# Score products on quarters of the TensorE array, without the quarters that the mask covers, and two fixed PSUM tiles for attention

## The chip, the cores and the metric

The kernel runs on one core of one Trainium2 chip. The metric is the device time of one execution in microseconds; lower is better. The five engines of the core are called as the profile calls them: PE (TensorE, the matmuls; PEld is its weight loads), DVE (VectorE), ACT (ScalarE), POOL (GpSimd) and SP (SyncE, which here only issues DMAs).

A matmul on PE has two instructions. A weight load puts the stationary operand into the array, which has 128 rows (the contraction) and 128 columns (the partitions of the result); the matmul then streams the moving operand through it, column by column, and the result goes to PSUM, which has banks of 512 f32 per partition. `tile_position=(r, c)` places a product smaller than the array at row r and column c.

## The reference

Four layers in a row on one sequence of 2048 rows of 640 numbers: attention, feed-forward, attention, feed-forward, with the same weights both times. Attention has 32 heads of 20 numbers, and a query sees itself and the 255 keys before it:

```python
scores = jnp.einsum("bhqd,bhkd->bhqk", q, k) * (Dh ** -0.5)
mask = (idx[:, None] - idx[None, :] >= 0) & (idx[:, None] - idx[None, :] < W)   # W = 256
scores = jnp.where(mask[None, None], scores, -1e9)
p = _softmax(scores, axis=-1)
o = jnp.einsum("bhqk,bhkd->bhqd", p, v)
```

Each layer takes a layernorm of x and adds its result to x. The feed-forward is `relu(x @ w1 + b1) ** 2 @ w2 + b2`, with 1536 inner columns. All of it is f32.

## The kernel before

**Units and quads.** The 2048 rows are cut into 8 units of 256 rows (T), and the two attention layers make 16 units (NU), numbered u = 0 to 15; units 0 and 8 are the first of a layer and have no unit of keys before them. Within a unit, four heads make a quad (NQ = 8 quads a unit, 128 in all). A unit's queries see keys of their own unit and of the one before. The 256 rows are two blocks of 128, so keys come in four blocks: kb = 0, 1 of the unit before, 2, 3 of its own.

**Numbers in two halves.** f32 operands are split into two f16 parts (high and low), and the products high x high, high x low and low x high are added. In the large products this is three matmuls into one accumulator (`mm3`, L256). In the scores the three terms lie below each other in the contraction: 3 x 20 = 60 rows. So a score product fills only half of the array's rows, and a quad's four heads are laid out as two pairs: e = 0 on rows 0 to 63, e = 1 on rows 64 to 127, and j = 0, 1 for the two heads that share a half.

**The steps of a quad.**
- `max_quad` (L499 to L537) makes the maxima. For each of four windows w = 2 j + i (a head pair j and a block i of 128 queries) the queries are the weights and 384 keys stream past, for e = 0 and 1 (L523). The result, 128 queries x 384 keys, goes to the tile bb[e]: windows 0, 1, 2 to the first 384 columns of banks 0, 1, 2, window 3 to the last 128 columns of all three banks. The keys come from the tile of the unit before (`prev`) and of this unit (`cur`), so a window is two matmuls, window 3 three. DVE then adds the mask `maskb` and takes the row maximum (L535, eight times a quad). In a layer's first unit only the unit's own keys are there.
- `max_out` (L541 to L565) turns the maxima of two quads with a transpose on PE (L547), and DMAs them into two more rows of the query tile, so that the next product subtracts them: 62 rows.
- `exp_quad` (L570 to L624) makes the scores again, transposed: a block of 128 keys is the weights and 128 or 256 queries stream past (L585), for each step of `steps_of` (L626): key block 1 with both query blocks, key blocks 0 and 3 with one each, key block 2 with both. A step is one bank of bb[e] with up to 512 columns. ACT takes the exponent of the bank into `pt` (L598), and POOL sets the masked half of the blocks to zero (L613, L617).
- `pv_quad` (L633 to L668) multiplies by the values, four heads on four strips of 32 array columns (L647), in f32.

**The banks.** The two tiles bb (three banks each) serve the maxima and the exponents in turn. `banks()` (L494) is called at the start of each block: it lets the planner's clock pass until the jobs that read them are due to be done (`need(*bbjobs)`), and asks the pool for two tiles with `bufs=2`, which come to lie on the same two places each time. The code's framework sets the semaphores for them from what reads and writes which tile.

**The order of the work.** The order of instructions on each engine is that of the program, set by a planner written in the kernel: it counts an estimated clock `now[0]`, in which a score block of `max_quad` or `exp_quad` costs 870 ns, and posts jobs of DVE, ACT, POOL and SP (`post`, `pump`) when their inputs are due. `together` spreads a unit's score blocks and value products among the large products of the neighbouring units (the projections, wo, and the feed-forward, all at L256, called dense work here), so that PE goes through one list: dense work, a maximum block, the value products of another quad, dense work, an exponent block, dense work. In the last unit (u = 15) less dense work is left to put between.

Of the kernel before, what the change touches and what calls it, by code (L numbers as in the profile page):

```python
# [10 lines left out]
F32 = mybir.dt.float32  # L11
# [5 lines left out]
P = 128  # L17
# [4 lines left out]
DH = 20  # L22
# [22 lines left out]
def kernel(ctx: ExitStack, tc: tile.TileContext, x, wqkv, wo, w1, b1, w2, b2, out):  # L45
    nc = tc.nc
# [4 lines left out]
    ps = ctx.enter_context(tc.tile_pool(name="ps", bufs=1, space=bass.MemoryType.PSUM))  # L51
# [68 lines left out]
    def post(eng, cost, fn, *deps, wait=0.0, prio=1, **kw):  # L120

        j = Job(eng, cost, fn, [d for d in deps if d is not None], now[0] + wait, prio, **kw)
        k = len(pend)
        while k and pend[k - 1].prio > prio:
            k -= 1
        pend.insert(k, j)
        return j
# [18 lines left out]
    def pass_time():  # L146
        now[0] = max(now[0], min(k.start() for k in pend if k.ready()) - LOOK)
        pump()

    def need(*js):  # L150

        for j in js:
            while j.end is None:
                pass_time()
            now[0] = max(now[0], j.end)
# [174 lines left out]
    def ln_t(u, yT=None):  # L330
        ys = lns.pop(u)
        if yT is None:
            yT = sb.tile([P, 2, KC, T], F16, name="yT", tag="yT", bufs=1)
        yTs[u], pre[u] = yT, []
        bb = banks() if u == 0 else (None, None)
        for i in range(2):
            yield from split_t(ys[i][0], yT[:, :, :, i * P:(i + 1) * P], ys[i][1], pre[u], bb[i])
# [151 lines left out]
    GQ = NQ // 4  # L489
    mxs = {}  # L490

    bbjobs = []

    def banks():  # L494
        need(*bbjobs)
        bbjobs.clear()
        return [ps.tile([P, 3, 512], F32, name="bb", tag="bb", bufs=2) for e in range(2)]

    def max_quad(n):  # L499

        u, qd = divmod(n, NQ)
        g = u % NG
        qt, cur, prev = qts[u], kts[u % 3], kts[(u - 1) % 3]
        G = qd // GQ
        if (u, G) not in mxs:
            mxs[u, G] = sb.tile([P, 2, 2 * GQ, 2], F32, name="mx", bufs=2)
        mx = mxs[u, G]
        need(trips[u, 0, qd], trips[u, 1, qd])
        bb = banks()

        for w in (3, 0, 1, 2):
            j, i = divmod(w, 2)
            p = 2 * qd + j
            parts = [(prev, 0, T, 0), (cur, 0, P, T)] if i == 0 else [(prev, P, T, 0), (cur, 0, T, P)]
            if g == 0:
                parts = parts[1:]
            if w == 3:
                parts = [(kt, z, z + P, c + z - a) for kt, a, b, c in parts for z in range(a, b, P)]
            for kt, a, b, c in parts:
                for e in range(2):  # L520
                    r = slice(64 * e, 64 * e + 3 * DH)
                    to = bb[e][:, c // P, 3 * P:] if w == 3 else bb[e][:, w, c:c + b - a]
                    nc.tensor.matmul(to, qt[r, p, i * P:(i + 1) * P], kt[r, p, a:b], start=True, stop=True)  # L523
        now[0] += 870.0 if g else 440.0
        for w in range(4):
            j, i = divmod(w, 2)
            o = (0 if g else T if i == 0 else P)
            for e in range(2):
                accum = mx[:, e, (2 * qd + j) % (2 * GQ), i:i + 1]
                if w == 3:  # L530
                    v, mask = bb[e][:, o // P:, 3 * P:], maskb[:, o:].rearrange("p (a n) -> p a n", n=P)
                else:
                    v, mask = bb[e][:, w, o:3 * P], maskb[:, o:]
                bbjobs.append(post("D", 113 + 1.047 * (3 * P - o), lambda v=v, mask=mask, accum=accum:
                                   nc.vector.tensor_tensor_reduce(out=v, in0=v, in1=mask, scale=1.0, scalar=-3.0e38,  # L535
                                                                  op0=ALU.add, op1=ALU.max, accum_out=accum)))
        mxjobs[u, G] = list(bbjobs)  # L537
# [32 lines left out]
    def exp_quad(n):  # L570

        u, qd = divmod(n, NQ)
        qt = qts[u]
        bb = banks()
        steps = steps_of(u)
        if qd % GQ == 0:
            need(rowjobs.pop((u, qd // GQ)))
        for k, st in enumerate(steps):
            o = 0
            for kb, kt, ko, q0, qn in st:  # L580
                w = qn * P
                for j in range(2):
                    for e in range(2):
                        r = slice(64 * e, 64 * e + 3 * DH + 2)
                        nc.tensor.matmul(bb[e][:, k, o:o + w], kt[r, 2 * qd + j, ko:ko + P],  # L585
                                         qt[r, 2 * qd + j, q0 * P:q0 * P + w], start=True, stop=True)
                    o += w
        now[0] += 870.0 if u % NG else 530.0
        out, masks = [], []
        for k, st in enumerate(steps):  # L590
            pts, ms = [], []
            for e in range(2):
                o = sum(2 * qn * P for _, _, _, _, qn in st)
                box = {}

                def power(k=k, e=e, o=o, box=box):
                    box["pt"] = sb.tile([P, 512], F32, name="pt", tag="pt", bufs=6)
                    nc.scalar.activation(box["pt"][:, :o], bb[e][:, k, :o], AF.Exp, scale=SCALE / (QS * QS))  # L598

                ex = post("A", 50 + 0.834 * o, power)  # L600
                bbjobs.append(ex)
                o2 = 0
                for kb, kt, ko, q0, qn in st:
                    w = qn * P
                    part = slice(o2, o2 + 2 * w)
                    o2 += 2 * w

                    def mask(box=box, part=part, kb=kb, w=w):
                        pj = box["pt"][:, part].rearrange("p (j n) -> p j n", j=2)
                        if kb < 2:  # L610

                            m = pj[:, :, w - P:w]
                            nc.gpsimd.affine_select(out=m, in_=m, pattern=[[0, 2], [-1, P]],  # L613
                                                    compare_op=ALU.is_gt, fill=0.0, base=0, channel_multiplier=1)
                        else:
                            m = pj[:, :, 0:P]
                            nc.gpsimd.affine_select(out=m, in_=m, pattern=[[0, 2], [1, P]],  # L617
                                                    compare_op=ALU.is_ge, fill=0.0, base=0, channel_multiplier=-1)

                    ms.append(post("G", 375, mask, ex))  # L620
                    pts.append((e, kb, q0, qn, box, part))
            out.append(pts)
            masks.append(ms)
        return out, masks  # L624

    def steps_of(u):  # L626

        cur, prev = kts[u % 3], kts[(u - 1) % 3]
        if u % NG == 0:
            return [[(2, cur, 0, 0, 2)], [(3, cur, P, 1, 1)]]  # L630
        return [[(1, prev, P, 0, 2)], [(0, prev, 0, 0, 1), (3, cur, P, 1, 1)], [(2, cur, 0, 0, 2)]]
# [276 lines left out]
    def together(ns, ms, dense, cost, share=1.0, whole=True, after=None, pace=0):  # L908
# [5 lines left out]
        for k, (part_, what, m) in enumerate(ts):  # L914
            if what and what[0] == "s":
                quad = exp_quad(what[1])
                for it in late:
                    max_out(*it)
                late.clear()
            if m is not None:  # L920
                max_quad(m)
                if m % GQ == GQ - 1:
                    late.append((m // NQ, m % NQ // GQ))
            if what and what[0] == "v":
                pv_quad(what[1], quad)
            if after and k == 0:
                after()
            part += part_
            while done < cost * share * part / total:
                c = next(dense, None)  # L930
                if c is None:
                    break
                step(c)
                done += c
            if what is None:
                for it in late:
                    max_out(*it)
                late.clear()
# [114 lines left out]
```

## Time and profile before

| what | value |
|---|---|
| median of 3 runs | 1659.74 us (1657.5 to 1660.65) |
| span of the profiled execution, first to last instruction | 1660.5 us |
| PE busy | 1595.4 us, 96% of the span |
| mean granted TensorE clock | 0.986 |
| dense matmuls at L256 on the chain that ended last | 65% of the span |
| value products at L647 on it | 10% |
| exponent score products at L585 on it | 6% |
| maximum score products at L523 on it | 5% |

The profile is one execution on the chip; it gives no time of its own beside the span, and the span lies within the runs' times. PE's busy time counts matmuls that overlap once, and the ends of matmuls are modelled, so the argument goes by the starts of instructions in the timeline and not by busy shares. A row of the timeline merges instructions of one line that follow each other: start in us, length in us from the first start to the last end, engine, line, operation, out<-in, shape, and xcount. A row of the groups has the count, then the busy time in us, the mean length of one in ns, and the engine's idle time before them with what ended it.

### The profile page before, as it was taken

The page shows a single profiled execution, that of the slowest core. Times are in us where ns is not written, and L with a number is a line of the kernel's source. Part 1 is how long each engine was busy: PE and PEld are TensorE (multiplying, and loading weights), DVE is VectorE, ACT ScalarE, POOL GpSimd, SP SyncE. Part 2 cuts the span into 40 slices and gives each one's busy share as a digit, 9 for nine tenths or more (in the row PEclk, how much of TensorE's full clock was granted, in tenths as well). Part 3 has the DMA queues.
Part 4 walks back from the last instruction along what each step waited for, and adds up shares of the span by engine and source line. Part 5 has one row for each costly group of instructions (what it writes and reads, how often), then busy time and mean ns, then how long its engine had stood idle before and what let it go on. Part 6 is the DMA issues. An engine that isn't in the chain of part 4 may idle for free.

```text
span 1660.5 us, 44547 instructions
## 1 busy us (share of the span) xinstructions
PE 1595.4 (96%) x17574; PEld 1173.0 (71%) x17574; DVE 1032.8 (62%) x3231; ACT 750.1 (45%) x1616; POOL 636.8 (38%) x1309
## 2 busy tenths in 40 slices
PE   7787899999999999999999999999999999999989
PEld 5564676777777777777777777777777777776667
DVE  7566657675665766566565756657665666757341
ACT  4455534535444454544434354444545444453512
POOL 1343533524344353424414243443534344353512
PEclk9897999999999999999999999999999999999999
DMA  8465214343452534335153433424343352421020
GB/s 245 129 179 155 61 61 107 63 118 84 100 101 60 125 69 113 78 102 118 50 136 74 123 82 104 98 68 118 73 109 80 104 115 50 108 70 53 26 64 17
DMA packets 231484, 157.42 MB, mean 95 GB/s; under 512 B 79468, under 2 KB 215020, under 8 KB 231276
## 3 DMA queue, kind: packets, MB, share of 16 engines
q1 hardware_dynamic: 231276, 154.59, 37.8%
q8 instruction: 138, 2.26, 0.6%
q14 instruction: 70, 0.57, 0.1%
HBM read 84.68 MB, written 52.95 MB: 83 GB/s over the span
## 4 chain that ended last, share of the span: by engine, by line
PE 87%; DVE 5%; ACT 3%; DMA 3%; issue 1%; SPq 1%; POOL 0%; DVEq 0%; ACTq 0%; POOLq 0%
PE acc L256 65%; PE pv L647 10%; PE bb L585 6%; PE bb L523 5%; DVE bb L535 2%; ACT pt L598 2%; DMA qk<-qd 1%; PE tr L547 1%; DMA qk<-yl 0%; DMA w_s<-in_A_wqkv_dram 0%; DVE mx L535 0%; DMA ov<-o 0%; DMA qt<-qk 0%; ACT r L816 0%; SPq L560 0%
## 5 line engine op out<-in xcount | busy, mean ns | idle before, releaser
L535 DVE CUSTOM_DVE_ANT_0 bb<-bb,maskb 128x384 f32<-128x384 f32 (+2 forms) x1024 | 510.4, 565 | 117.3 <-PE bb L523 109.4
L598 ACT ACTIVATE pt<-bb 128x512 f32<-128x512 f32 (+1 forms) x736 | 376.5, 602 | 239.9 <-PE bb L585 239.6
L613 POOL TENSOR_SCALAR_AFFINE_SELECT pt<-pt 128x256 f32<-128x256 f32 x448 | 195.0, 440 | 542.8 <-ACT pt L598 521.4
L256 PE MATMUL acc<-y,w_s 128*128 128x256 f16 x2880 | 331.8, 273 | 4.2 <-DVE y L304 1.4
L256 PE MATMUL acc<-w_s,hh 128*128 128x320 f16 x2304 | 326.2, 299 | 0.0
L256 PEld LDWEIGHTS <-w_s 128*128 128x128 f16 x2880 | 278.5, 98 | 58.2 <-issue 25.7
L256 PE MATMUL acc<-yT,wq_s 128*128 128x256 f16 x2400 | 282.7, 276 | 12.6 <-DVE qd L414 10.6
L256 PEld LDWEIGHTS <-hh 128*128 128x128 f16 x2304 | 221.8, 98 | 97.8 <-issue 15.3
L256 PEld LDWEIGHTS <-wq_s 128*128 128x128 f16 x2400 | 233.7, 99 | 58.0 <-issue 27.8
L617 POOL TENSOR_SCALAR_AFFINE_SELECT pt<-pt 128x256 f32<-128x256 f32 x512 | 217.1, 446 | 64.3 <-ACT pt L598 63.2
L826 DVE TENSOR_TENSOR hh<-r,hh 128x256 f16<-128x256 f32 x192 | 91.7, 499 | 208.4 <-ACT hh L823 200.9
L647 PE MATMUL pv<-pt,vt 128*32 128x128 f32 (+1 forms) x3840 | 188.8, 331 | 2.0 <-POOL pt L617 1.4
L820 POOL TENSOR_TENSOR r<-r 128x256 f32<-128x256 f32 x192 | 113.5, 612 | 184.9 <-ACT r L816 183.4
L659 ACT COPY ot<-pv 128x256 f32<-128x256 f32 x128 | 47.6, 372 | 285.6 <-PE pv L647 285.6
L535 DVE DVE_READ_ACCUMULATOR2_ANT mx<- 128x1 f32 x1024 | 142.7, 139 | 0.1
L256 PE MATMUL acc<-wq_s,yT 128*128 128x320 f16 x960 | 142.0, 301 | 0.1
L647 PEld LDWEIGHTS pv<-pt,vt 128*32 128x32 f32 x3840 | 104.2, 110 | 49.1 <-issue 17.6
L256 PE MATMUL acc<-wo_s,od 128*128 128x320 f16 x900 | 131.9, 301 | 3.6 <-DVE x L758 1.7
L816 ACT ACTIVATE r<-acc,b1s 128x256 f32<-128x256 f32 x192 | 80.6, 471 | 99.8 <-PE acc L256 98.4
L256 PEld LDWEIGHTS <-yT 128*128 128x128 f16 x960 | 93.0, 98 | 40.4 <-issue 7.0
L585 PE MATMUL bb<-qt,kt 62*128 62x128 f16 (+1 forms) x1920 | 109.4, 246 | 10.6 <-DVE mx L535 9.8
L256 PEld LDWEIGHTS <-od 128*128 128x128 f16 x900 | 86.1, 98 | 45.9 <-issue 11.1
(84 smaller groups left out, 1175.7 us busy)
## 6 DMA issues: line engine op xcount, KB each, us to landing
qt<-qk SPq DMA_DIRECT2D x30, 480.0 KB
kt<-qk SPq DMA_DIRECT2D x30, 480.0 KB
qk<-qd SPq DMA_DIRECT2D x17, 640.0 KB
o<-ot SPq DMA_DIRECT2D x256, 42.0 KB
od<-o SPq DMA_DIRECT2D x13, 640.0 KB
qk<-yl SPq DMA_DIRECT2D x13, 640.0 KB
qk<-qd SPq DMA_DIRECT2D x17, 320.0 KB
xt<-in_A_x_dram SPq DMA_DIRECT2D x16, 320.0 KB
```

The lines of the kernel that those rows point to most:

```text
L256: nc.tensor.matmul(acc, lhs(a, c), rhs(b, c), start=(k == 0), stop=(k == 3 * nk - 1))
L523: nc.tensor.matmul(to, qt[r, p, i * P:(i + 1) * P], kt[r, p, a:b], start=True, stop=True)
L535: nc.vector.tensor_tensor_reduce(out=v, in0=v, in1=mask, scale=1.0, scalar=-3.0e38, op0=ALU.add, op1=ALU.max, accum_out=accum)))
L585: nc.tensor.matmul(bb[e][:, k, o:o + w], kt[r, 2 * qd + j, ko:ko + P], qt[r, 2 * qd + j, q0 * P:q0 * P + w], start=True, stop=True)
L598: nc.scalar.activation(box["pt"][:, :o], bb[e][:, k, :o], AF.Exp, scale=SCALE / (QS * QS))
L613: nc.gpsimd.affine_select(out=m, in_=m, pattern=[[0, 2], [-1, P]], compare_op=ALU.is_gt, fill=0.0, base=0, channel_multiplier=1)
L617: nc.gpsimd.affine_select(out=m, in_=m, pattern=[[0, 2], [1, P]], compare_op=ALU.is_ge, fill=0.0, base=0, channel_multiplier=-1)
L647: nc.tensor.matmul(pv[32 * jj:32 * (jj + 1), q0 * P:(q0 + qn) * P], vf[:, c:c + 32], pj[:, j, :], start=(k == 0), stop=(k == len(steps) - ...
L659: nc.scalar.copy(ot[:, qd % 2], pv)
L816: nc.scalar.activation(box["r"], acc[:, f, :], AF.Relu, bias=b1s[:, f0 + f:f0 + f + 1], scale=1.0 / (YS * WS))
L820: nc.gpsimd.tensor_tensor(box["r"], box["r"], box["r"], op=ALU.mult)
L826: nc.vector.tensor_sub(hh[:, 1, f, :], box["r"], hh[:, 0, f, :])
```

## The change

A score product now fills a quarter of the array: rows by e as before, and columns by a new half h = 0, 1. In `max_quad` h is a half of the 128 queries; in `exp_quad` it is a half of the 128 keys. Each quarter is a weight load of 64 columns and a matmul of its own, at `tile_position=(64 * e, 64 * h)`, whose result goes to 64 of the 128 partitions of bb[e].

From unit 2 on each half streams only what the mask leaves for some row of it. In `max_quad` the first 64 queries of a block see the first 320 of the window's 384 keys, the others the last 320. In `exp_quad` a half of a key block of the unit before (kb < 2) leaves out the last 64 queries if h = 0, and a half of a key block of its own unit leaves out the first 64 if h = 1. Units 0 and 1 are written whole. What is not written keeps what an earlier block left there; the mask of DVE and the zeros of POOL cover it as before.

`by_turns` orders the matmuls of the two halves: the next one comes from the half that has streamed fewer columns so far, and each is issued for e = 0 and e = 1.

The two tiles bb are made once, before the loop, and `banks()` returns them each time. The estimates (870 ns) and all jobs of the other engines are as they were.

```diff
+    def by_turns(ways):
+        t = [0, 0]
+        ways = [list(w) for w in ways]
+        while ways[0] or ways[1]:
+            h = min((h for h in range(2) if ways[h]), key=lambda h: t[h])
+            part = ways[h].pop(0)
+            t[h] += part[0]
+            yield h, part
+
     bbjobs = []
+    bbs = [ps.tile([P, 3, 512], F32, name="bb", tag="bb", bufs=2) for e in range(2)]
 
     def banks():
         need(*bbjobs)
         bbjobs.clear()
-        return [ps.tile([P, 3, 512], F32, name="bb", tag="bb", bufs=2) for e in range(2)]
+        return bbs
...
+            ways = [[], []]
             for kt, a, b, c in parts:
+                for h in range(2):
+                    lo, hi = (0, 3 * P) if u < 2 else (64 * h, 64 * h + 320)
+                    x, y = max(a, a + lo - c), min(b, a + hi - c)
+                    if x < y:
+                        ways[h].append((y - x, kt, x, y, c + x - a))
+            for h, (_, kt, a, b, c) in by_turns(ways):
                 for e in range(2):
-                    r = slice(64 * e, 64 * e + 3 * DH)
-                    to = bb[e][:, c // P, 3 * P:] if w == 3 else bb[e][:, w, c:c + b - a]
-                    nc.tensor.matmul(to, qt[r, p, i * P:(i + 1) * P], kt[r, p, a:b], start=True, stop=True)
+                    r, m = slice(64 * e, 64 * e + 3 * DH), slice(64 * h, 64 * h + 64)
+                    to = bb[e][m, c // P, 3 * P + c % P:3 * P + c % P + b - a] if w == 3 else bb[e][m, w, c:c + b - a]
+                    nc.tensor.matmul(to, qt[r, p, i * P + 64 * h:i * P + 64 * h + 64], kt[r, p, a:b],
+                                     start=True, stop=True, tile_position=(64 * e, 64 * h))
...
+        ways = [[], []]
         for k, st in enumerate(steps):
             o = 0
             for kb, kt, ko, q0, qn in st:
                 w = qn * P
                 for j in range(2):
-                    for e in range(2):
-                        r = slice(64 * e, 64 * e + 3 * DH + 2)
-                        nc.tensor.matmul(bb[e][:, k, o:o + w], kt[r, 2 * qd + j, ko:ko + P],
-                                         qt[r, 2 * qd + j, q0 * P:q0 * P + w], start=True, stop=True)
+                    for h in range(2):
+                        a, b = 0, w
+                        if u >= 2:
+                            a, b = (0, w - 64 * (1 - h)) if kb < 2 else (64 * h, w)
+                        ways[h].append((b - a, kt, 2 * qd + j, ko, q0 * P + a, k, o + a))
                     o += w
+        for h, (w, kt, p, ko, q, k, o) in by_turns(ways):
+            for e in range(2):
+                r = slice(64 * e, 64 * e + 3 * DH + 2)
+                nc.tensor.matmul(bb[e][64 * h:64 * h + 64, k, o:o + w], kt[r, p, ko + 64 * h:ko + 64 * h + 64],
+                                 qt[r, p, q:q + w], start=True, stop=True, tile_position=(64 * e, 64 * h))
```

## The prediction

> **What bounds the kernel now.** I read the shares and the chain on the page first, then the span cut into stretches, then single blocks in the timeline.
>
> ```profile
> span 1660.5 us, 44547 instructions
> ...
> PE 1595.4 (96%) x17574; PEld 1173.0 (71%) x17574; DVE 1032.8 (62%) x3231; ACT 750.1 (45%) x1616; POOL 636.8 (38%) x1309
> ...
> PE 87%; DVE 5%; ACT 3%; DMA 3%; issue 1%; SPq 1%; POOL 0%; DVEq 0%; ACTq 0%; POOLq 0%
> PE acc L256 65%; PE pv L647 10%; PE bb L585 6%; PE bb L523 5%; DVE bb L535 2%; ACT pt L598 2%; DMA qk<-qd 1%; PE tr L547 1%; DMA qk<-yl 0%; DMA w_s<-in_A_wqkv_dram 0%; DVE mx L535 0%; DMA ov<-o 0%; DMA qt<-qk 0%; ACT r L816 0%; SPq L560 0%
> ```
> ```profile
> 200.00:900.00 700.00, 695.88 (x7876) 516.08 (x7876) 445.99 (x1419) 319.20 (x697) 275.67 (x586) 1.00 0.39 92
> 900.00:1428.00 528.00, 526.91 (x6003) 390.35 (x6001) 346.53 (x1065) 240.19 (x517) 207.16 (x441) 1.00 0.39 93
> 1428.00:1574.00 146.00, 136.93 (x1596) 96.69 (x1595) 87.25 (x282) 68.48 (x152) 66.19 (x139) 0.99 0.24 60
> ```
> In the table of stretches the columns are length, then busy time of PE, PEld, DVE, ACT and POOL, granted clock, DMA share and GB/s. From 200 to 1428 us PE is busy 1222.8 of 1228 us at full clock: there PE is the limit, and a nanosecond taken off a score block is a nanosecond off the span, because PE works through one list in order. The two score blocks that the change rewrites (L585 and L523) are only 11% of the chain, some 180 us.
>
> ```profile
> 603.49 0.84 PE L523 MATMUL bb<-kt,qt 60*128 60x128 f16 x18
> 604.26 1.51 PE L647 MATMUL pv<-pt,vt 128*32 128x256 f32 x32
> ...
> 607.89 2.34 PE L256 MATMUL acc<-w_s,hh 128*128 128x320 f16 x16
> ...
> 610.16 0.83 PE L585 MATMUL bb<-qt,kt 62*128 62x256 f16 x16
> ...
> 610.93 5.06 PE L256 MATMUL acc<-w_s,hh 128*128 128x320 f16 x36
> ```
> ```profile
> L256 PE MATMUL acc<-w_s,hh 128*128 128x320 f16 x2304 | 326.2, 299 | 0.0
> L647 PE MATMUL pv<-pt,vt 128*32 128x256 f32 x1920 | 154.3, 388 | 0.3
> ```
> Sixteen 320-column matmuls take 2.34 us, and the last one's own length is 0.30, so they start (2.34 - 0.30) / 15 = 0.136 us apart: **0.425 ns per column**. A maximum block sends 4 x 384 = 1536 columns through each of its two row halves, an exponent block 6 x 256 = 1536. That is 0.653 us of streaming, if the halves run together. The timeline has the next work starting 0.77 us after either block starts (603.49 to 604.26, 610.16 to 610.93). The halves do run together: one after the other they would need 1.31 us. Streaming sets the block, and some 0.12 us go to its start and to the change of the array's division.
>
> **The change, part by part.** *Columns.* From unit 2 on, a query half needs 320 of 384 keys and a key half 192 of 256 queries (or 64 of 128) in a masked piece. Each quarter then streams 4 x 320 = 1280 columns, and an exponent quarter 512 + 384 + 384 = 1280 as well. That is 256 fewer per quarter, 256 x 0.425 = 109 ns per block. It holds where a block spans two key units: units 2 to 7 and 9 to 15, 13 x 8 = 104 quads, 208 blocks. Units 0 and 1 are written in full. In unit 8 one half keeps all its 768 columns while the other drops to 512, and the longer half sets the end. So 48 blocks (24 quads) gain nothing.
>
> *Instructions.* The 2176 matmuls of L523 become 4352 and the 1920 of L585 become 3840, each with its weight load: 36 for 18 and 32 for 16 in a full block. Four must run at once for the time above, and every load must hide behind the matmul before it in its own quarter. No row has such a quarter; the nearest ones are these.
>
> ```profile
> 604.26 0.42 PE L647 MATMUL pv<-pt,vt 128*32 128x256 f32 x4
> ```
> ```profile
> L523 PEld LDWEIGHTS <-qt 60*128 60x128 f16 x2176 | 72.7, 95 | 38.9 <-issue 35.7 <-DMA w_s<-in_A_wo_dram 0.3
> L647 PEld LDWEIGHTS pv<-pt,vt 128*32 128x32 f32 x3840 | 104.2, 110 | 49.1 <-issue 17.6 <-POOL pt L617 6.5 <-POOL r L820 1.9
> L300 PEld LDWEIGHTS tr<-ident,xt 128*128 128x128 f32 x50 | 5.5, 140 | 9.7 <-issue 3.5 <-DVE yT L304 1.8 <-ACT vt L480 1.7
> L547 PEld LDWEIGHTS tr<-ident,mx 128*16 128x16 f32 x64 | 5.6, 87 | 13.8 <-issue 8.8 <-DVE yl L414 2.9 <-PE acc L256 0.6
> ```
> *Four at once.* Four value products on four column strips span 0.42 us when one lasts 0.39: they start about 10 ns apart and overlap. Column strips overlap there, row halves overlap in the score blocks; both together is my assumption. A group of four that starts one by one costs some 15 ns more than today's pair at each block's start.
>
> *Loads.* Loads of 16 and 128 columns last 87 and 140 ns, so 53 / 112 = 0.47 ns per column over a fixed 79.5. That fixed part is latency. The 128-column f16 load has 95 - 79.5 = 15.5 ns beyond it, a fourth of what 0.47 would make, so today's loads take a quick form. The 32-column load on a strip has 110 - 79.5 = 30.5, which is 0.95 per column, twice the rate, but on f32. For 64 f16 columns the ends are therefore 64 x 0.12 = 8 ns and 64 x 0.95 = 61 ns; 0.47 gives 30. I take **30 ns**: the strip's row is nearer in its division of the array, but its f32 operand is wider, and the whole-array pair brackets 64 columns without that. At 30 ns the loads hide behind matmuls of 128 columns and more (54 ns) and barely fail behind those of 64 (27 ns). [...]
>
> *Sum.* A trimmed block: -109 + 15 + 15 + 20 = -59 ns; times 208 is -12.3 us. An untrimmed one: +15 + 15 + 10 for the order, times 48 is +1.9 us. Net **-10.4 us**.
>
> *Fixed banks.* The two bb tiles already fall on the same two buffers at every call, and the planner's clock (870 ns a block) and its list are untouched, so the order of emission stays.
>
> ```profile
> PE bb L585 <- DVE mx L535: 9.8, 10, 3.5
> ...
> PE bb L523 <- ACT pt L598: 4.3, 10, 1.2
> ```
> All waits of PE for the banks (columns: us, times, longest) are 14.1 us in 20 places. The first products into a bank still need its readers gone, and the last maximum of a quad (w = 3) reads all three banks. I put the gain at 0; the ends are -14 (all gone) and some +2 us, if more semaphores have to be asked for. DVE and ACT keep every instruction; they start when a block ends, earlier by what it saves, and the next score block comes earlier by as much, so their slack stays. Should DVE's eight maxima become late, the same bank wait grows.
>
> 1660.5 - 10.4 = 1650.1. The median, 1659.74, lies 0.8 us below the profiled span, within the 3.2 us between the runs; I say **1650.5 us**.
>
> **The rivals.**
> (a) *The load sets the pace* (slower). At 61 ns a quarter's nine matmuls in a maximum block (128, 128, 64, 256, 64, 128, 192, 256, 64 columns) cost six times 61 and 109, 82, 109, so 666 ns, and 61 for the first load: 727 + 15 against 668 today, +74. [...] It decides from a load of about 36 ns, where the 109 ns are used up. For it: the strip's row. Against it: the 16 and 128 column rows.
> (b) *The gain is used up.* A load of 33 to 39 ns, or some more cost at the start: 1660, within 0.2% either way.
> (c) *A floor per matmul, or quarters that take turns.* The closest steady spacing in the block row is 18 in 0.65 us, so about 36 ns, or 27 within its 128-column run. With 27 as a floor, 36 matmuls need 0.97 us and 32 need 0.86: some +0.25 us for each of 256 blocks, +64 us, 1725. Halves that took turns would add more still. Against it: four strip products started within 0.03 us. [...]
> (d) *Better than forecast.* Loads as quick as today's: -109 + 15 per trimmed block, -18 us in all, or the bank waits gone on top of the forecast: 1638 to 1643.
>
> **How the numbers follow.** Forecast 48%, (a) 21%, (b) 12%, (c) 10%, (d) 9%. A measurement here tells about 0.2%, 3.3 us, from no change. Faster: the forecast and (d), 0.57. Same: (b), 0.12. Slower: (a) and (c), 0.31. The forecast's own range, with a load of 27 to 33 ns, is 1646 to 1656. The 8-in-10 range runs from 1639, in (d), through the likeliest, (b) and most of (a), to 1690; it leaves out (c) and the edges of (a) and (d).
>
> **What will show it.** 4352 and 3840 score matmuls in the groups. The new loads' mean, less 79.5: 30 right, 50 or more means (a), 15 means (d). Start of a block to start of what follows: 0.71 us instead of 0.77 in units 2 and later, 0.81 in unit 1. Span from 200 to 1428 us down by some 10, as much as the blocks' sum; if the blocks shrink and the span doesn't, PE waits elsewhere and my one-to-one rule is wrong. The waits for DVE mx and ACT pt near 14 us. What would make all this wrong: four quarters not running at once.

## The result, and the profile after

The changed kernel takes 1642.91 us (median of 4 runs, 1641.93 to 1644.1) against 1659.74 (1657.5 to 1660.65). The ratio is 0.9899 with a 95% interval of 0.9885 to 0.9913: 16.8 us faster. The forecast was 1650.5, 9.2 us faster. The sign held, and the time lies in the stated range of 1639 to 1690, but near its lower end and outside the forecast's own range of 1646 to 1656: the gain is larger than the sum behind it.

The page of the changed kernel, the same lines as before:

```profile
span 1640.2 us, 52819 instructions
...
PE 1575.6 (96%) x21670; PEld 1172.6 (71%) x21670; DVE 1030.1 (63%) x3231; ACT 748.4 (46%) x1616; POOL 636.6 (39%) x1309
...
PE 83%; DVE 6%; ACT 4%; DMA 4%; POOL 2%; issue 1%; SPq 1%; DVEq 0%; ACTq 0%; POOLq 0%
```

PE has 4096 matmuls and as many weight loads more, and is busy 20 us less. DVE, ACT and POOL kept their counts. The table of stretches (length, then busy time of PE, PEld, DVE, ACT, POOL, granted clock, DMA share, GB/s) and the list of what PE waited for (us, times, longest):

```profile
200.00:900.00 700.00, 696.42 (x9795) 521.90 (x9793) 450.61 (x1439) 319.71 (x699) 275.43 (x584) 1.00 0.39 93
900.00:1428.00 528.00, 526.25 (x7608) 394.35 (x7606) 351.80 (x1086) 242.80 (x524) 208.93 (x447) 1.00 0.41 97
```
```profile
PE bb L613 <- DVE mx L555: 8.4, 11, 3.0
...
PE bb L542 <- ACT pt L625: 4.5, 10, 1.2
```

PE is as full as before (1222.7 of 1228 us): it is still the limit, and the same list passes in less time. The bank waits are 12.9 us in 21 places, against 14.1 in 20. So the gain is not in waits but in the blocks themselves. The timeline of PE in unit 6, where L523 is now L542 and L585 is L613:

```profile
631.61 0.76 PE L542 MATMUL bb<-kt,qt 60*64 60x128 f16 x36
632.29 1.51 PE L674 MATMUL pv<-pt,vt 128*32 128x256 f32 x32
...
637.65 0.75 PE L613 MATMUL bb<-qt,kt 62*64 62x192 f16 x32
638.34 0.28 PE L567 MATMUL tr<-ident,mx 128*16 128x128 f32 x1
```

From the start of a block to the start of what follows it takes 0.68 and 0.69 us, where it took 0.77. To the nanosecond of the trace the medians over units 2 to 7 and 9 to 14 (96 blocks of each kind) are 766 before and 685 after for both kinds, and a block also begins 3 ns sooner after the matmul ahead of it: **84 ns per trimmed block**.

The stage in which PE is the limit can be cut out cleanly, between the first exponent block of unit 2 and that of unit 15. Before:

```profile
238.14 0.28 PE L585 MATMUL bb<-qt,kt 62*128 62x256 f16 x1
```
```profile
1500.02 0.28 PE L585 MATMUL bb<-qt,kt 62*128 62x256 f16 x2
```
After:

```profile
234.24 0.27 PE L613 MATMUL bb<-qt,kt 62*64 62x192 f16 x1
```
```profile
1481.92 0.30 PE L613 MATMUL bb<-qt,kt 62*64 62x192 f16 x4
```

That stage took 1261.9 us and takes 1247.7: **14.2 us** of the gain. It came out the same to 0.1 us in two profiles of the changed kernel and 1.0 us apart in the widest pair of one program (e7_unit1 and e12_unit1 below), while the start of the kernel scatters by 2 us and the runs by 3; so the experiments below are read by it first and by their medians second. Its 192 trimmed blocks of 84 ns make 16.1 us. Three things take most of the difference: unit 8's 16 blocks are 13 to 20 ns longer (0.3 us), blocks that held a wait before shrink by less (0.7 us), and dense work now waits for DVE's reading of the transposed maxima, a wait that the stage of before does not have (0.9 us in this profile, 0.5 in the second one):

```profile
PE acc L256 <- DVE mT L573: 0.9, 3, 0.4
```

### The profile page after: what moved, and what is told of

It is laid out like the page before. It is cut to its first block, busy times and chain, and to the rows that moved or that the text cites. A ratio compares the mean times of both kernels' runs of the same rounds, so it can differ in the third digit from the quotient of the medians.

```text
span 1640.2 us, 52819 instructions
## 1 busy us (share of the span) xinstructions
PE 1575.6 (96%) x21670; PEld 1172.6 (71%) x21670; DVE 1030.1 (63%) x3231; ACT 748.4 (46%) x1616; POOL 636.6 (39%) x1309
## 4 chain that ended last, share of the span: by engine, by line
PE 83%; DVE 6%; ACT 4%; DMA 4%; POOL 2%; issue 1%; SPq 1%; DVEq 0%; ACTq 0%; POOLq 0%
PE acc L256 63%; PE pv L674 10%; PE bb L542 5%; PE bb L613 5%; DVE bb L555 3%; ACT pt L625 2%; DMA qk<-qd 1%; DMA xt<-in_B_b_dram 1%; PE tr L567 1%; POOL x L805 1%; DVE mx L555 1%; POOL pt L644 0%; ACT r L843 0%; DMA w_s<-in_B_w_dram 0%; DMA ov<-o 0%
## 5 line engine op out<-in xcount | busy, mean ns | idle before, releaser
L843 ACT ACTIVATE r<-acc,b1s 128x256 f32<-128x256 f32 x192 | 80.6, 471 | 98.0 <-PE acc L256 97.2
L613 PE MATMUL bb<-qt,kt 62*64 62x128 f16 (+3 forms) x3840 | 100.3, 235 | 9.1 <-DVE mx L555 8.4
```

Of the source, the lines that this page charges most:

```text
L613: nc.tensor.matmul(bb[e][64 * h:64 * h + 64, k, o:o + w], kt[r, p, ko + 64 * h:ko + 64 * h + 64], qt[r, p, q:q + w], start=True, stop=True ...
L843: nc.scalar.activation(box["r"], acc[:, f, :], AF.Relu, bias=b1s[:, f0 + f:f0 + f + 1], scale=1.0 / (YS * WS))
```

## The experiments

Each run was timed beside the kernel before on the same chip. "Stage" is the stretch just named.

| run | median, us | ratio to before (95%) | stage, us |
|---|---|---|---|
| before | 1659.7 to 1660.6 | 1 | 1261.9 |
| the change | 1642.9 | 0.9899 (0.9885 to 0.9913) | 1247.7 |
| e1_banks | 1660.1 | 0.9997 (0.9987 to 1.0007) | 1261.9 |
| e2_whole | 1663.1 | 1.0017 (1.0009 to 1.0026) | 1266.3 |
| e3_max_only | 1651.5 | 0.9947 (0.9933 to 0.9961) | 1255.6 |
| e4_exp_only | 1650.6 | 0.9944 (0.9931 to 0.9957) | 1254.7 |
| e5_cut64 | 1683.6 | 1.0138 (1.0123 to 1.0154) | 1282.3 |
| e6_in_turn | 1674.6 | 1.0078 (1.0064 to 1.0093) | 1271.4 |
| e7_unit1 | 1645.2 | 0.9904 (0.9890 to 0.9917) | 1249.6 |
| e8_estimate | 1650.0 | 0.9935 (0.9923 to 0.9948) | 1248.6 |
| e9_plain_order | 1643.3 | 0.9900 (0.9885 to 0.9916) | 1247.7 |
| e10_estimate950 | 1646.9 | 0.9917 (0.9904 to 0.9930) | 1246.1 |
| e11_changed | 1644.3 | 0.9909 (0.9892 to 0.9925) | 1247.7 |
| e12_unit1 | 1643.4 | 0.9903 (0.9888 to 0.9917) | 1248.7 |

### The fixed banks alone

```diff
+    bbs = [ps.tile([P, 3, 512], F32, name="bb", tag="bb", bufs=2) for e in range(2)]
...
-        return [ps.tile([P, 3, 512], F32, name="bb", tag="bb", bufs=2) for e in range(2)]
+        return bbs
```

> The kernel before with the two fixed bank tiles alone; all products as before. Theory (the gain is the columns that are not streamed, banks nothing): no change, within 1.5 us of before, the waits of PE for DVE mx and ACT pt still near 14 us. Rival (the fixed tiles let matmuls start before the last reader of the other banks is done): 5 to 14 us faster, and those waits shrink by as much.

The median and the stage are those of before. What PE waited for in this run:

```profile
PE bb L587 <- DVE mx L537: 9.3, 12, 3.0
...
PE bb L525 <- ACT pt L600: 4.4, 10, 1.2
```

13.7 us in 22 places: nothing moved. The rival is out, and all of the gain belongs to the products.

### Quarters without the trimming

```diff
-                    lo, hi = (0, 3 * P) if u < 2 else (64 * h, 64 * h + 320)
+                    lo, hi = 0, 3 * P
...
-                        if u >= 2:
-                            a, b = (0, w - 64 * (1 - h)) if kb < 2 else (64 * h, w)
```

> The changed kernel, with the quarters but without the trimming: every half streams all keys and queries in every unit. Theory: the division costs what it costs in unit 1 of the changed kernel, +44 ns for a maximum block and +20 ns for an exponent block, so about +32 ns for 256 blocks, 6 to 8 us slower than before (1666 to 1668). Rival (dividing the array is itself quicker, for instance by a shorter drain): faster than before, by up to half of the 16.8 us.

2.8 us slower than before (1.5 to 4.3). Dividing the array does cost, and nothing of the gain comes from it. It costs less than I expected: two blocks of this run, in PE's timeline,

```profile
622.49 0.85 PE L611 MATMUL bb<-qt,kt 62*64 62x256 f16 x32
623.28 0.28 PE L567 MATMUL tr<-ident,mx 128*16 128x128 f32 x1
...
628.37 0.86 PE L542 MATMUL bb<-kt,qt 60*64 60x128 f16 x36
629.16 1.08 PE L672 MATMUL pv<-pt,vt 128*32 128x256 f32 x24
```

take 0.79 us each (medians 787 and 786 ns), 20 more than before for both kinds. The +44 ns in my expectation was the median of the eight maximum blocks of unit 1 of the changed kernel. Four of them took 787 ns there too; the others took 882 to 1427 ns, and the two longest ran while the granted clock was 0.50. Against this run the trimming alone shortens a block from 787 to 685, 102 ns of the 109 that its columns make, and the stage by 18.6 us.

### One kind of block at a time

Each of these has the new code in one function, and the old lines in the other.

> The maxima in trimmed quarters, the exponent products as before. Theory: 104 blocks shorter by 84 ns and 24 longer by some 30, so 8 us faster than before (1652), half of the whole gain. Rival (the chain through the banks is the limit, so a shorter maximum block only makes the exponent block wait for DVE): less than 4 us.

> The exponent products in trimmed quarters, the maxima as before. Theory: 104 blocks shorter by 84 ns and 24 longer by some 20, so 8 us faster than before (1651); with the run of the maxima alone it adds up to the whole 16.8 us within 2. Rival: the two do not add up, because the bank waits take up a part of either.

In the stage the maxima bring 6.3 us and the exponents 7.2, together 13.5 of the 14.2; by the medians 8.7 and 9.7, together a little over the whole. They add up, so neither block's gain is eaten by a wait that the other would have to lift, and the chain through the banks is not the limit.

### Where the price of a block comes from

Two runs change only what is issued, not what is streamed. In the first, every piece is cut to 64 columns:

```diff
-                        ways[h].append((y - x, kt, x, y, c + x - a))
+                        ways[h] += [(64, kt, z, z + 64, c + z - a) for z in range(x, y, 64)]
```
(and likewise in `exp_quad`).

> The changed kernel with every score matmul cut into pieces of 64 columns, so twice and more as many weight loads and matmuls for the same columns: 20 pieces a quarter in a trimmed block. If a 64-column load takes 27 ns or less, it hides behind 64 columns (27.2 ns) and blocks stay at 685 ns, 1643 to 1645 in all. If it takes 29 ns with its issue, a trimmed block is some 35 to 40 ns longer, 1652 to 1654 in all. If the strip's rate (61 ns) held, or a floor of 27 ns per matmul, a block would grow by 0.6 us or more, over 1780.

Some 40 us slower than the changed kernel, between the cases of the expectation. The timeline has most blocks like the first one here, and some like the second:

```profile
635.96 0.84 PE L542 MATMUL bb<-kt,qt 60*64 60x64 f16 x80
636.74 0.72 PE L674 MATMUL pv<-pt,vt 128*32 128x256 f32 x9
```
```profile
796.96 0.47 PE L542 MATMUL bb<-kt,qt 60*64 60x64 f16 x34
799.23 0.81 PE L542 MATMUL bb<-kt,qt 60*64 60x64 f16 x46 [1.79 <-issue]
```

A typical maximum block takes 773 ns, 88 more than in the changed kernel, against the 35 to 40 that I expected for a load of 29 ns. In the first block a quarter passes 20 pieces; the last one's own length is 0.19, so they start (0.84 - 0.19 - 0.03 for the first load) / 19, some 32 ns apart, where 64 columns stream in 27. So streaming does not set the pace here. The load with its issue, at some 32 ns and not 61, is what fits, but no run separates it from another cost of a short matmul. The loads' own rows of the changed kernel come close, 109 and 107 less the fixed 79.5, so 27.5 to 29.5 ns:

```profile
L542 PEld LDWEIGHTS <-qt 60*64 60x64 f16 x4352 | 72.2, 109 | 36.5 <-issue 35.5 <-DMA w_s<-in_A_wo_dram 0.3 <-DMA xt<-in_A_x_dram 0.2
L613 PEld LDWEIGHTS <-kt 62*64 62x64 f16 x3840 | 70.1, 107 | 43.5 <-issue 39.2 <-DMA o<-ot 1.3 <-DMA xt<-xs 1.1
```

Eighty matmuls in 0.65 us is also 8 ns per matmul: the floor of 27 ns of rival (c) does not exist in this form.

The second block stops for 1.8 us in its middle without waiting for a semaphore. Of the 96 maximum blocks of units 2 to 7 and 9 to 14, 26 take over 0.8 us from their start to the next work and 8 over 1.2, six of these by such a stop. The program's PE list is half again as long here (33062 matmuls for 21670), and the instruction queue q8 moved 259 packets for 170. Over the whole run PE stops ten times inside a score block for 0.6 to 1.8 us with nothing to wait for, and each time it goes on 1.3 to 1.5 us after a packet of 16 KB of that queue had ended. What held it, no run was made to show.

In the second run, all matmuls of one half come first:

```diff
-            h = min((h for h in range(2) if ways[h]), key=lambda h: t[h])
+            h = 0 if ways[0] else 1
```

> The changed kernel, but the matmuls of the half h = 0 all come before those of h = 1 (within a window in the maxima, within the block in the exponents). Theory (the gain needs both halves in the array at once, and matmuls start in order): a trimmed maximum block +0.24 us, an exponent block +0.43, some 75 to 80 us in all, 1715 to 1725, slower than before. Rival (the array reorders, so that the order of issue does not matter): as the changed kernel, 1643.

Some 31 us slower than the changed kernel, so both halves at once is what the gain needs, but less than half of what I expected. A maximum block has 698 ns instead of 685, an exponent block 936. The timeline shows why. PE's matmuls that started in the first 30 ns of a maximum block of this run:

```profile
635.29 0.24 PE L542 MATMUL bb<-kt,qt 60*64 60x128 f16 x4
```

The same four by their columns:

```profile
L542 PE MATMUL bb<-kt,qt x4: 213/226/240, 635.3 to 635.3; 60*64 60x128 f16 x2, 60*64 60x64 f16 x2
```

In the program the first window has pieces of 128, 128 and 64 columns for h = 0, and behind them 64, 128 and 128 for h = 1, each for e = 0 and 1. Two matmuls of 128 and two of 64 have started, so the two of 64 were ahead of two of 128 that stand before them in the program. **Matmuls of different quarters did not start in the order of the program** in this run. In the exponent block one half is 16 matmuls ahead: 192, 192, 64, 64, 128, 128, 256 and 256 columns for h = 0, each for e = 0 and 1, and behind them 256 for h = 1. Its first 0.27 us, by columns:

```profile
L613 PE MATMUL bb<-qt,kt x12: 189/230/293, 666.4 to 666.6; 62*64 62x192 f16 x4, 62*64 62x64 f16 x4, 62*64 62x128 f16 x2, 62*64 62x256 f16 x2
```

The 256 columns of h = 1 start when ten of the sixteen of h = 0 have, ahead of six others. For the rest the halves run partly in turn: the block is 251 ns longer than the 685 of the changed kernel, where I had expected 430.

That makes the balance of `by_turns` doubtful, so in one more version the halves simply alternate:

```diff
-            t[h] += part[0]
+            t[h] += 1
```

> The changed kernel with the two halves simply in turn, one matmul pair of h = 0, one of h = 1, without the balance of columns. Theory from the run with one half after the other (there a matmul of h = 1 started before matmuls of h = 0 that came earlier in the program, so a quarter does not wait for the others within some matmuls): the balance is worth nothing, trimmed blocks stay within 10 ns of 685 and the time within 1.5 us of the changed kernel. Rival (matmuls start in order, as the prediction had it): some 50 ns more for each trimmed block, 10 us slower than the changed kernel.

> The changed kernel itself again, beside the three below on the same chip: 0.99 of before, 1642 to 1645 us. It is what they are compared with.

Both take 685 ns for a block, 1247.7 us for the stage and, within their scatter, the same time. A typical maximum block and a typical exponent block of the two runs start their matmuls at the same nanoseconds after the block's start, to within one, though the programs have them in different orders. So in these blocks no quarter lost time to the place of its matmuls in the program: of the term that I had put down for the order, these runs show nothing.

### Unit 1, and the planner's estimate

Unit 1 is written whole because the banks hold nothing before it. From its second quad on they do:

```diff
-                    lo, hi = (0, 3 * P) if u < 2 else (64 * h, 64 * h + 320)
+                    lo, hi = (0, 3 * P) if n <= NQ else (64 * h, 64 * h + 320)
```
(and `n > NQ` for `u >= 2` in `exp_quad`).

> The changed kernel, trimmed in unit 1 too from its second quad on (the first quad of unit 1 has written all banks by then). Theory: 7 maximum and 7 exponent blocks go from 834 and 786 to 685 ns, so 1.7 us faster than the changed kernel, if PE is the limit there; rival: unit 1 waits for DMA and converted weights, and nothing is gained.

> Unit 1 trimmed too, again. Theory after the first run (unit 1's blocks shrank from 834 and 786 to 783 and 684 ns, and unit 2 began at 234.1 us as in the changed kernel): units 0 and 1 are not limited by PE, so no gain, within 1 us of the changed kernel. Rival: the 1 to 1.7 us that the blocks save, hidden by scatter in the first run.

No gain, in either: 1643.4 beside 1644.3 for the changed kernel on the same chip, with runs that overlap. Unit 2 begins at 234.1 and 235.4 us, in the changed kernel at 234.2 and 236.0. Units 0 and 1 are not limited by PE (in the changed kernel it is busy 148.2 us of the 180 between 50 and 230 us). So a longer block costs nothing that shows there, and a shorter one brings nothing. The two stages are 1.9 and 1.0 us longer than the changed kernel's, and the wait of dense work for the transposed maxima is longer in them, 2.9 and 1.7 us; in e7_unit1:

```profile
PE acc L256 <- DVE mT L573: 2.9, 4, 1.1
```

> The changed kernel with the planner's estimate of a full score block set to 790 ns instead of 870 (460 and 550 in a layer's first unit). Theory: the estimate only sets when jobs are posted; within 2 us of the changed kernel. Rival: the planner's clock runs slow against PE by 80 ns a block, and a right one takes waits away: 3 to 6 us faster.

> The changed kernel with the planner's estimate of a full score block at 950 ns (480 and 580 in a layer's first unit). At 790 ns it lost 7 us, 6 of them before unit 2 began. Theory: that start hangs on the order in which the planner puts weight conversions beside score blocks, and any other estimate only shuffles it: from the third unit on within 1 us of the changed kernel, the start different by several us either way. Rival: a higher estimate leaves more slack and gains 3 us or more.

The blocks have the same lengths in both, and the stage is 1248.6 and 1246.1 us. But the first exponent block of unit 2 comes late:

```profile
240.14 0.27 PE L613 MATMUL bb<-qt,kt 62*64 62x192 f16 x1
```
```profile
241.03 0.27 PE L613 MATMUL bb<-qt,kt 62*64 62x192 f16 x1
```

at 240.1 with 790 ns and at 241.0 with 950 ns, against 234.1 to 236.0 in the five profiles with quarters and trimming in both blocks that keep 870 and the balance or plain order (the changed kernel and unit 1 twice each, plain order). A truer estimate is not a better one. With 790 ns PE waits 5.2 us at the start for ACT (`r`, L843), a wait that the changed kernel does not show, so the order of the work there has a part in it. The granted clock between 50 and 230 us is lower as well, 0.89 and 0.88 against 0.90, and no run separates the two. No version clearly faster than the changed kernel was found. 870 ns in units 0 and 1 with 950 behind them could give the 1.6 us of the stage, little more than the 1.0 by which the stage of one program differs; it was not tried.

## Why the prediction was right, and where its sizes were off

- **PE is the limit, and a block's saving is the span's.** Right. PE stayed full at 1222.7 of 1228 us, the halves of the gain add up (e3, e4), and 16.1 us of block time became 14.2 of stage.
- **The columns.** 256 fewer per trimmed block at 0.425 ns, 109 ns. Right: e2 against the changed kernel gives 102.
- **The price of the division.** This is the term that was mis-sized: "-109 + 15 + 15 + 20 = -59 ns" for a trimmed block measured -84, so a price of 25 and not 50. The 15 + 15 for the first load (30 less the 15.5 of before) and four starts measured 18 (e2: 21 ns longer, begun 3 sooner). The load's part was about right, 12 to 14 by its rows of 107 and 109 beside the 95 of before; the 15 for four starts was too much: they start within some 10 ns of each other, as the pair did within 3. The 20 for 64-column matmuls is shown by no run: the 109 of the columns less the 102 of e2 against the changed kernel leave 7. The 20 counted on matmuls that start in the program's order, so that one half waits for the other. That was not shown either: in e6 two matmuls started ahead of two that stand before them, and two ahead of six, and e9, with another order, had the starts of the changed kernel to within 1 ns. Over the stage the prediction's sizes make 192 x 59 - 16 x 40 ns, so 10.7 us; it measured 14.2.
- **The load.** Taken as 30 ns between the ends 8 and 61; its rows give 27.5 to 29.5 beyond the 79.5, and some 32 with its issue fit the pace of e5. Right, and it was the number on which the sign hung. A load of 64 columns on a quarter takes, beyond the 79.5, nearly twice the 15.5 ns that one of 128 columns took before.
- **Untrimmed blocks.** Put at +40 ns for 48 blocks, +1.9 us. They cost 20 (e2), no run shows the 10 for the order that is in the 40, and most of them lie in units 0 and 1, where PE is not the limit (e7, e12): nothing to add for those. So the sum should have been about 192 to 208 trimmed blocks of 84 ns, 16 to 17 us. That this is close to the median's 16.8 is partly luck, since the stage shows 14.2 of it, and no run ties the rest to the blocks.
- **From the sum to the forecast.** 10.4 us off the median of 1659.74 is 1649.3. The 1650.5 on record is 1.2 us above it and has no reason beside it.
- **The banks.** 0, and measured 0 (e1).
- **The rivals.** (a) and (b) fell with the load. (c) fell with e5 (matmuls 8 ns apart), and quarters do run four at once, which no row of before had shown: the first four of a block start within some 10 ns, where 128 columns alone stream in 54. (d) named the right time, 1638 to 1643, for a wrong reason: neither quicker loads nor lost waits.
- **What stays open.** The stage leaves 2.6 us of the median's 16.8. Between the two profiles the span shrank by 20.3 us: 3.9 before the stage, 14.2 in it, 2.2 behind it. The first exponent block of unit 2 came at 238.1 us in both profiles with the old products and 2 to 4 us sooner in those of the changed kernel, though unit 0's and 1's blocks are longer. Behind the stage 160.5 us became 158.3, but e2, without the trimming, has 158.2 too. Start and end scatter, and no run was made to explain them.

## What to carry to other kernels

Where small products fill half of the array's rows, look whether half of its columns lets you leave out work as well. Here a load of 64 columns, 27.5 to 29.5 ns beyond the fixed 79.5, is shorter than the 54 ns in which 128 columns stream, and in blocks that have matmuls of 64 columns too, 102 of the 109 ns of the columns left out were gained. Price such a block by its own fixed costs (here 20 to 25 ns for the division), and then count it only in the stages where that engine is the limit. A stage cut out between two marks in the trace shows differences of 2 us that the 3 us between whole runs would hide.

## What the runs showed of the hardware that was not expected

- Matmuls on different quarters of the array did not keep to the order of the program: in e6 two started ahead of two, and two ahead of six, that stand before them. Two runs with different orders (e9, e11) had the same starts to within a nanosecond in a typical block. In e6 a block with one half ahead by four or six matmuls lost 13 ns, one with a half ahead by 16 lost 251.
- In e5 matmuls with a weight load each started 8 ns apart on average over a whole block of 80 (0.65 us).
- In e5 PE stopped ten times for 0.6 to 1.8 us inside score blocks of a program with half again as many PE instructions, with nothing to wait for in the profile, and went on 1.3 to 1.5 us after a packet of the instruction queue each time.
